# A recorded order of 2471 operations replaced by another: sliding-window attention and a token-mixing MLP on one core

## Chip, core and metric

The kernel runs on one NeuronCore of a Trainium2 chip. The metric is device time in microseconds (us), the median over several runs. The engines are named as the profile names them: PE (TensorE, matmuls; PEld its weight loads), DVE (VectorE), ACT (ScalarE), POOL (GpSimd) and SP (SyncE, whose queue issues every DMA here).

## What is computed

The input x is 2048 tokens of 512 features. The program runs two layers; each is an attention block and then a token-mixing MLP, both with a residual.

```python
def A(x):    # 32 heads of 16, window 256
    q, k, v = split(x @ wqkv)
    p = softmax(where(0 <= i - j < 256, q @ k.T / 4, -1e9))
    return (p @ v) @ wo
def B(x):    # mixes tokens: 2048 -> 1792 -> 2048, per feature
    u = gelu(einsum("sd,sf->df", layernorm(x), w1) + b1)
    return (einsum("df,fs->ds", u, w2) + b2).T
for _ in range(2):
    x = x + A(layernorm(x))
    x = x + B(layernorm(x))
```

## The kernel before

**Recording and replay.** The program isn't issued as it is written. Each call of `op(...)` puts an operation with its tiles, its engine and its possible other engines (`alts`) into a graph (L107 to L148). `replay` (L175) then goes through a list that `begin_order` decodes from the string `ORDER`: each entry names the operation that is next and which of its alternatives is used. The entries of one engine, in that sequence, are that engine's instruction stream; buffers of the pools (eight PSUM banks, seven `pt` tiles, and so on) are handed out in the same sequence. `emit` (L196) puts in the semaphore waits. So the string alone sets the order on every queue and the choice of engine.

**Work of a layer.** Tokens go in 16 tiles of 128. For each tile DVE takes statistics (`stat` L470, `agg` L472), POOL the power -0.5 (`rstd`, L483), and DVE normalises (`xh`, L490). The result is transposed into `xhT`: for the first four tiles on PE (`ftr`, L548) with a copy out of PSUM (`evt`, L555 on DVE or L557 on ACT), for the others by DMA (`tr`, L541). Projections are groups of matmuls on L512 (`fq`, `fk`, `fv`), evicted as `evq` (L571/L573), `evk` to a staging tile (L593/L595), `evka` straight into the block-diagonal keys `kbd` with two instructions (L582/L581), and `evv` (L630/L632). Staged keys are spread into `kbd` by `kz` on POOL or DVE (L608, two instructions) or by eight DMAs (L603). `kbd` has to be zero elsewhere: POOL fills two of its three slots at the start (`zero`, L460, 128x2048 each).

**Attention** goes over 152 groups of scores, 76 a layer. A group is `sc` on PE (L689, four row groups at once, two pairs of PSUM banks), two `exp` on ACT (L704, one for each pair of banks), up to a few `mask` operations on the edge blocks (L725: on POOL a product with `ldm`, on DVE an AND with `ldn`), and, once the groups of an output are there, `pv` (L746). The output is transposed by DVE (`od` L766), its reciprocal taken (`rec` L770), multiplied (`prod` L772, POOL or DVE), transposed back (`od2` L777), and goes through `fwo` (L512) and the residual `res` (L788).

**MLP.** `fu` (L512) and `ful` (L867) are the first product, part of it run during attention on the tokens that are ready; `evu` (L852/L854/L856) and `addu` (L878) gather it, `gelu` is on ACT (L882), `fy` (L512) is the second product and `resy` (L908, L894) its residual. Weights w1 and w2 stream in by DMAs of 128 KB (L802, L814).

**Start.** Before the first scores: POOL builds `ident`, `tri`, `mhalf`, sets the ones of `vst` (`one`, L457) and makes the two zero fills; PE runs 42 warm-up matmuls (L393); two tiles of x are normalised (`xh[48]` and `xh[44]`, the numbers being places in the recording), transposed (`ftr[51]`, `ftr[49]`), copied (`evt[52]` on ACT, `evt[50]` on DVE), and the first keys and queries are made from them (`fk[53]`, `fq[55]`), evicted, and used by `sc[113]`.

Of the kernel before, what the change touches and what calls it, by code (L numbers as in the profile page):

```python
# [14 lines left out]
ORDER = (
    'c-pO2F^KC{7QM2c=j(6YfM!uZS>AxMXh91KD2oCLD4;@F9MA^^T)0r-!i5VL+TcP9VsW7bFL*%#7cNvd;KGFiUhskg4!D?wSul$i9GJqz6cd=jg^MYsm|ga2'
    'Jmc}qpHF_Wku6K_>b<9X&b{|s3((~u28fD9C#cz^(P&uU6DaxBQmLft&MVz<4C52s)D1{l?kfP#BbAEk)EtMLm&@L%<IYdr`FswtJTWaWnS9KcJW&)X%U3)b'
    '@oN$VXI3W(lMXv3@d>4I%QDizq2cv9>WB4uy%I)YSkW{}gD9vq>L!28TupO`S}dvsCNn}ri4aOgJQ0AvsIVN~Twl`}&!;{9^74}Kq!YK3a=9Eg8-gHgmceFy'
    'IzQ!$hqIY|wmNgV7VtcOrO4Ci{CY93R1|+Un<+dGQaVk0-Sv8{5tW>uM^LW=gD@;NW{t+|L{*(?L05D#==IaVkT{g4N!s0bZQ>T<RvgO-fgk|UthU>2k>_hv'
    '4CixFCNo;ENu*Y<5yvSzm1<==^$2031}XbxJKjvzgTXZDo1Ry#_C9eeJ4#HyVtbzMnw5`Vxuw$l=5yEkcw?HbXCf-e)K$|mNyfw^XIaD1Xb6M%4bwE=6-7Y+'  # L20
    '_!A)@Nm8RB1|s8Yc+Yssxvn5O%h7Ua7=}<J7Z>odP|&otrnl#9nE}8N_=l9zUKB-e4M`G)n@vbzy^f;q&YEXu-=)!I=Q4rZ$;E25`p3yhr_(8~PCU;rPEJlw'
    '=imNrKCjme`+QoReLbDe|Fx0j>DfR$!&lbk^IF$5jHHt!ecy=VP8=Hsa`l%ujxDRzZbfmdP^yO!6;;<&#j0K1SY{b>k)HE>7@f(>KLnVLrCO~7P{z{%r#Nt3'
    '*XvT6fQ^Sl=@%dH(i{OxM3{^x;^+tvk|I*Z+O6YOb_hZn_$H=1GUn6*{IyIlN+rjkwHl>J1g~p~Q*?`(q`-!;%L~(zR%-ykWI$)b8G#Al-tS_D%ZhxMBnc!2'
    'XXw!&62kQ5;b8$-Gm=9lm(WdICkSS-$T?EIQYC(=EQ*SPg@Q49?>+R6ke9#+yY@F5K<b4fSfTYu)8?7)yeJ;RXhg?o8VrOq6$Pn7kJ`{$E-sMe>;*6x00*Nq'
    'P5W2<6hPB-LflfdR0)E*2QuaZRKfRjQ7eI7)K#E7D4>d00$4IwV#QyY5+HWw01WM++aD81hgLdBv1lw$FSgxw9P5#8=tiwrtGfnoFEvXyHQl3f*-&)e_g5o+'
    '2<^T^#Y!aF7&$2nf;0_+K&mTojG;0RO_2@(e4lBW<}##E#WQA2N|JCeX!qM~gwfW<@wf?ptA<KX5HPC~{1uCmbmUvU5Joy<S-kC9pjVH8RBP2MzQanq@ba_I'
    'sPHKpIQ?~>je#tPX%WN1go}m5Fn(M7upYMR1efCJ6<qUur)YSdXFI0tSg0@}pyp^AC-BI<KnZ>CrXf<QYU%|XsjJlj@6M6&nW|0H$%Ov~j&V&^Z?QNW27*fI'
    'g<4iCP3=FMjnjd{?|D9oczo{rd>Nn=ND^F0P`SDyqCgm<LV;f{m;8m5Z8BLdmes|g*PG24Ti7<UrWoDv`0L43f?o=r09=~(`n^t?{;Hkef_}e`jzS+ruzPiN'
    'NgyKa^YbwLGnN!PJ!uHdFpxqi(?hW;3as1x-1q$!iy`pC(02prGo@0gmMs8_d_+Xz*ovZXAIa})SOo}F(*f}@e91xua(ar<5Cu9KjbON5Gr5zrTkX-Zuvjeq'
    '-9izTW2p%sigPdd0;G43L?M|ZtUVmcxJkoxU)A79Qhly)wm_G(6Yck!uviR-!^N_U^pJ1ymC<-KvVT1uL%)xD?eU!sm-bTBEdyM)*Xy-q`Kz|n9pVO^WYF*5'  # L30
    '+~~cYjM}YrP_kRCd5GbjhH(?@z_wAAA*=B!k+EyJD4dS%6X#;NbR3y7Lz+lgHZVt$W!b>O(J<9eFBletgQ6fvD2|MQC<zh@3_qR1f2W41>q9aa47--z{{S?A'
    'gwHBnYO@xI%>Wnh6`@!J-nA)~yP}8%;o`D?-tVto9+JbCol{il)_6L@#>;&b^?QgArd<jskV!BKf@UG=_njW<TG6jyEg^c#0NwWy4R%DgNHwjiqSZ81Lq*Q3'
    'Olq(?T;sl_Tiq#sf4RQAz%}|tpD*-(o}+4?pO#@Z|7J45Ed0AT9*;#$6Gy80Wil%JX;)0KmnDhv<zF$W|A?LlLIAZ|Eeu1;bY1L<m27LbWV?2W5P?ufvOh)5'
    '&_4u1jy3f+1D-D&3&N2g5YjAgz4L}5qc$~8qF@qanTibxFzr3d!DTDa!iFrK0?5<eB)wihD3M!5i^AK_WCTg4EcSw4(g>3v3F2~qVeeIYmeA>T{G?O$TT65#'
    'TjdmCP_%8wE|qC{<JG*HYc`7IYR#;am}Qub;y4%y-A2}Q^hFd!))`Yl6$IJtg2Ed-Ntq;<WUuDjR3v|MO*hsRZ#bSLuASM<+4Sa;v1^Gj;pY0n5n`jWT3wKH'
    '8p^V^-gs-*9Z;UkVbN?h75?Uikg>Ny&w6l*e=?>Rm$Bg)ktbA%R?`4mA8(q9!Rs=Rl7{NzWKwM-M@S396KO=wc=$;N$Ni`Y*&u6waPZ93gS|zs?MrUIcMtD&'
    '+D^=d`P&ix=JR*veE!7?ynFFt_vrp|dy-qj!R_>eH~O(19z3=lWZ&H=x4jg0)ARWp<Z=&Bb|i4mQd77?nj<-qLAk?~eRA9rF1QzO!}uE`u|LQkJh5i4<{n%<'
    'czEq|@5^Q1J%G7f2052|!pbg4<S8RRkS*L3=JHz$_tVioe-xgz=AX5q_grqz$J}jz9=Ws&Ajdt}x3-5M-i|ZAavb--`+Z*T;6K{-O~v-JvBAO5N-TZLS@ao}'
    'bK7*fKX#`5t#jL)yHCAbZok;zox&qvWE%j0ci!2L5#AAQA3i=HnaFeZQuB-ZX_+}wnL7o_uK9faK~M6qQ>Q(Z;W!>IkM$@2WY!kQ!=nczx&6v|HX9!ebGiN1'
    '2r~C5W1gv-+kS>_XNU<hL3Tp>-0{e~CEy-XeoICngH*`BRy~FMQ_G$qzr&x~2l5!@y(zb^HuuqoyM)<;`M8jND6_GQ?@Nz+b1mG>;db5UbxnVp3fgURmy)|p'  # L40
    '?p)yDuA^}e%Fpe~A@?Yx+v!^o;hqS{Pwo}@|EIxlZ}ne*dz&8hLut?b7{B(Y-v8t9aL?T_xn=)OB<^E@zqxy|cbdJO{#3f}^5XvTv#Rv{@jteS6(a'
)
# [945 lines left out]
```

## Time and profile before

| | us |
|---|---|
| median of 3 runs (439.57 to 442.05) | 440.72 |
| the profiled execution's own time | 439.72 |
| its span, first to last instruction | 438.0 |
| PE busy / DVE / ACT / POOL | 422.0 / 324.0 / 315.4 / 187.8 |
| first `exp` of layer 1 starts | 12.36 |
| last `exp` of layer 1 ends (its table load follows at once) | 156.3 |
| last `fy` matmuls | to 435.0 |

The span has five stretches. Up to 12.36 us the first tiles are made ready. To some 156 us is the attention of layer 1, with the early part of the MLP in between. To some 200 us is the rest of the MLP of layer 1. To 358 us is the attention of layer 2, mixed with the last `fy` of layer 1 and the early MLP of layer 2; the rest is the MLP of layer 2. PE's busy time counts a matmul from issue to its modelled end, so that neighbours overlap. An instruction on ACT that lasts 1.05 us lets the next start 0.90 us after it began; the difference is overlap too.

### The profile page before, as it was taken

Reading aid. Unit: us, or ns where it says so; the run is one execution under the profiler, and the core shown is the slowest. Engines: PE = TensorE matmul, PEld = TensorE weight load, DVE = VectorE, ACT = ScalarE, POOL = GpSimd, SP = SyncE. Lnnn points to the kernel's source line nnn. Section 1 sums busy time; section 2 is a strip of 40 time slices with the busy share of each in tenths; the row PEclk is TensorE's granted clock in tenths of the full one; section 3 lists DMA queues with packets and bytes.
Section 4 is the critical chain, followed back from the end, with each engine's and each line's share of the span. In section 5 each row is a group of like instructions: output and inputs, shape, how many; then the busy total and the mean of one; then the engine's idle time right before and its main releaser. Section 6 shows DMA issues by size and latency. Waiting matters only on the chain.

```text
span 438.0 us, 13924 instructions
## 1 busy us (share of the span) xinstructions
PE 422.0 (96%) x5976; PEld 187.2 (43%) x5976; DVE 324.0 (74%) x634; ACT 315.4 (72%) x360; POOL 187.8 (43%) x278
## 2 busy tenths in 40 slices
PE   6989988999989999999999999999999999999997
PEld 5543433333434444444344444444444444444443
DVE  6999888988988679565677999989888757520214
ACT  2999999999999932704989999999999980520000
POOL 6779976548582421010255554468556411000000
PEclk8999999999999999999999999999999999999999
DMA  8745552212252635643583152122324134668513
GB/s 235 151 88 76 136 100 65 67 22 55 46 131 54 165 84 169 180 123 85 143 127 86 36 131 69 22 62 41 73 50 121 53 100 131 192 187 244 159 36 120
DMA packets 106668, 46.13 MB, mean 105 GB/s; under 512 B 36848, under 2 KB 106608, under 8 KB 106608
## 3 DMA queue, kind: packets, MB, share of 16 engines
q1 hardware_dynamic: 106608, 45.26, 42.0%
q8 instruction: 47, 0.77, 0.8%
q14 instruction: 13, 0.11, 0.1%
HBM read 33.56 MB, written 2.10 MB: 81 GB/s over the span
## 4 chain that ended last, share of the span: by engine, by line
PE 81%; ACT 13%; DVE 4%; issue 1%; POOL 1%; DMA 0%
PE PS L512 56%; ACT pt L704 13%; PE PS L689 9%; PE PS L867 8%; PE PS L746 7%; DVE xh_sb L490 1%; DVE stats L470 1%; DVE x_sb L788 1%; DMA x_sb<-in_A_x_dram 0%; POOL pt L725 0%; DVE kbd L582 0%; DVE rl L766 0%; DVE agg L472 0%; DVE stg L593 0%; DVE qT L571 0%
## 5 line engine op out<-in xcount | busy, mean ns | idle before, releaser
L704 ACT ACTIVATE pt<-PS 128x1024 bf16<-128x1024 f32 (+1 forms) x304 | 280.6, 1039 | 9.8 <-PE PS L689 8.9
L725 POOL TENSOR_TENSOR pt<-pt,ldm 128x256 int32<-128x256 int32 (+2 forms) x195 | 130.5, 689 | 106.1 <-ACT pt L704 105.6
L512 PE MATMUL PS<-xhT,wqkv 128*128 128x512 bf16 (+1 forms) x288 | 68.2, 363 | 2.0 <-ACT pt L704 0.9
L512 PE MATMUL PS<-xh_sb,w1b 128*128 128x512 bf16 x280 | 69.6, 381 | 0.3 <-issue 0.2
L512 PE MATMUL PS<-uT,w2b 128*128 128x512 bf16 (+1 forms) x294 | 68.5, 370 | 0.0
L689 PE MATMUL PS<-qT,kbd 32*128 32x256 bf16 (+4 forms) x1488 | 60.4, 252 | 5.0 <-ACT pt L704 1.4
L908 DVE SCALAR_TENSOR_TENSOR x_sb<-PS,b2col,x_sb 128x512 bf16<-128x512 f32 x31 | 22.8, 745 | 43.7 <-PE PS L512 43.6
L483 POOL TENSOR_TENSOR rstd<-agg,mhalf 128x2 f32<-128x2 f32 (+1 forms) x33 | 22.9, 695 | 63.4 <-DVE agg L472 63.3
L689 PEld LDWEIGHTS PS<-qT,kbd 32*128 32x128 bf16 x1488 | 21.9, 93 | 63.4 <-ACT pt L704 44.6
L766 DVE STREAM_TRANSPOSE rl<-PS 128x1024 f32<-128x1024 f32 x32 | 39.8, 1243 | 10.5 <-PE PS L746 10.5
L882 ACT ACTIVATE uT<-rl,b1col 128x512 bf16<-128x512 f32 x28 | 18.2, 712 | 38.5 <-DVE rl L878 38.3
L746 PE MATMUL PS<-pt,vb 64*17 64x320 bf16 (+4 forms) x2976 | 43.3, 252 | 1.6 <-POOL pt L725 0.6
L470 DVE BATCH_NORM_STATS2 stats<-x_sb 128x6 f32<-128x512 bf16 x64 | 42.9, 682 | 1.4 <-DMA x_sb<-in_A_x_dram 0.6
L512 PEld LDWEIGHTS PS<-uT,w2b 128*128 128x128 bf16 x294 | 27.1, 98 | 31.6 <-issue 3.7
L512 PE MATMUL PS<-uT,pt 128*128 128x512 bf16 x168 | 40.4, 380 | 0.0
L725 DVE TENSOR_TENSOR pt<-pt,ldn 128x256 int32<-128x256 int32 (+1 forms) x75 | 28.7, 404 | 15.7 <-ACT pt L704 15.5
L746 PEld LDWEIGHTS PS<-pt,vb 64*17 64x17 bf16 x2976 | 30.8, 85 | 17.7 <-ACT pt L704 6.1
L867 PE MATMUL PS<-xh_sb,w1b 128*128 128x512 bf16 x168 | 37.7, 379 | 0.0
L512 PEld LDWEIGHTS PS<-xhT,wqkv 128*128 128x128 bf16 x288 | 24.6, 99 | 29.7 <-issue 5.6
L512 PEld LDWEIGHTS PS<-xh_sb,w1b 128*128 128x128 bf16 x280 | 23.4, 97 | 31.9 <-issue 7.2
L512 PE MATMUL PS<-wqkv,xhT 128*128 128x512 bf16 x128 | 34.1, 381 | 0.0
L512 PE MATMUL PS<-wo_sb,oT 128*128 128x512 bf16 x128 | 32.3, 380 | 0.7 <-ACT pt L704 0.5
(61 smaller groups left out, 338.1 us busy)
## 6 DMA issues: line engine op xcount, KB each, us to landing
w1b<-in_B_w_dram SPq DMA_DIRECT2D x112, 128.0 KB, 2.9
w2b<-in_B_w_dram SPq DMA_DIRECT2D x70, 128.0 KB, 2.9
pt<-in_B_w_dram SPq DMA_DIRECT2D x42, 128.0 KB, 2.8
vb<-vst SPq DMA_DIRECT2D x64, 68.0 KB, 2.1
out_dram<-x_sb SPq DMA_DIRECT2D x15, 128.0 KB, 1.8
x_sb<-in_A_x_dram SPq DMA_DIRECT2D x3, 512.0 KB, 7.5
kbd<-stg SPq DMA_DIRECT2D x88, 16.0 KB, 1.9
wqkv<-in_A_wqkv_dram SPq DMA_DIRECT2D x4, 256.0 KB, 4.2
```

The lines of the kernel that those rows point to most:

```text
L470: op("vector:stat", lambda e: e.bn_stats(st[:, 0:6], x_sb[:, t, :]), reads=[f"x{t}"], writes=[("st", i)], cost=dve_cost(512))
L483: op("gpsimd:rstd", lambda e: e.tensor_tensor(rstd[:, t0:t1, 0], agg[:, t0:t1, 1], mhalf[:, 0:1].to_broadcast([P, t1 - t0]), op=ALU.pow), ...
L490: op("vector:xh", lambda e: e.tensor_scalar(xh_sb[:, t, :], x_sb[:, t, :], agg[:, t, 0:1], rstd[:, t, :], op0=ALU.subtract, op1=ALU.mult), ...
L512: return e.matmul(o, lhsT=w, rhs=x, start=start, stop=stop, skip_group_check=True)
L689: last = e.matmul(bank(tt[r // 2], r % 2)[:, base + c0 * 64:base + (c0 + n) * 64], lhsT=kbd[32 * r:32 * r + 32, tk.slot, o, jj].rearrange( ...
L704: op("scalar:exp", lambda e, ts=ts, tp=tp, i=i, cols=cols: e.activation(probs(tp)[:, i, 0:cols, :], pair(ts)[:, :, 0:cols].rearrange("p r ...
L725: return e.tensor_tensor(v, v, m, op=by)
L746: last = e.matmul(bank(t, h)[32 * r:32 * r + 17, i + q0 * 64:i + (q0 + n) * 64], lhsT=vb[64 * h:64 * h + 64, tk.slot, jj, 4 * o + r, :], r ...
L766: op("vector:od", lambda e, t=tod, tr=tr: e.transpose(rl[:, tr.slot:tr.slot + 2].rearrange("p a b -> p (a b)"), pair(t)), reads=[(tod, i) ...
L867: last = e.matmul(bank(tu, tt), lhsT=v()[:, sc - b0, k0 + tt * P:k0 + (tt + 1) * P], rhs=xh_sb[:, sc, :], start=(sc == b0), stop=(sc == NT ...
L882: op("scalar:gelu", lambda e, ft=ft, tt=tt: e.activation(uT[:, ft, :], rl[:, tmps[tt].slot], ACTF.Gelu_apprx_tanh, bias=b1col[:, ft:ft + 1 ...
L908: op("vector:resy", lambda e: e.scalar_tensor_tensor(x_sb[:, t, :], bank(ft), b2col[:, t:t + 1], x_sb[:, t, :], op0=ALU.add, op1=ALU.add), ...
```

## The change

The string `ORDER` is replaced; nothing else in the file differs.

```diff
 ORDER = (
-    'c-pO2F^KC{7QM2c=j(6YfM!uZS>AxMXh91KD2oCLD4;@F9MA^^T)0r-!i5VL+TcP9VsW7bFL*%#7cNvd;KGFiUhskg4!D?wSul$i9GJqz6cd=jg^MYsm|ga2'
...
+    'c-p;JL5S<t6}_^b=Rdb^Km%_;1qJkr0t%=_0Tukg1%2?s1qbwt0}8m{g$fS1Ac|7F@WKHX6mUQb2efd(3oRV*!T~S5_zM?YaA7`p;l*D}VF)gG@fTjqVkood'
...
 )
```

Decoded, the two lists hold the same 2471 operations. The start of the two, engine by engine (`-` and a number in brackets are nameless set-up operations: 0 to 2 `ident`, 3 `mhalf`, 26 and 27 the memset and the select of `tri`, 28 to 33 the mask tables `ldm` and `ldn`, 22 to 25 `par` and `half`, 37 to 39 the constants of `stats`):

```
POOL before: -[0] -[3] -[1] -[2] zero[35] rstd[47] -[26] rstd[43] -[27] one[34] zero[36] kz[66] rstd[83] mask[121] kz[71] kz[76]
POOL after:  -[3] -[0] -[1] -[2] one[34] zero[35] rstd[47] rstd[43] -[26] -[27] zero[36] rstd[83] kz[66] mask[117] kz[71] kz[76]
DVE before:  ... xh[48] xh[44] -[28] -[29] evt[50] -[31] -[32] -[30] ldn[33] evq[56] stat[81] stat[79] evq[68] evk[75] agg[82] evk[70] agg[80] evq[78] xh[84] evq[73] xh[85] stat[160] stat[153] evv[62] evt[87] evt[89]
DVE after:   ... xh[48] -[39] xh[44] stat[79] evt[50] -[28] stat[81] -[29] agg[82] agg[80] -[31] -[30] xh[85] -[32] ldn[33] xh[84] evq[78] evt[89] evk[70] stat[153] stat[160] stat[162] evt[87] ... evv[59] -[20] evv[62]
ACT before:  evt[52] evka[54] evk[65] exp[114] exp[115] exp[120] exp[119] exp[124] exp[125] evv[59] 3 exp evq[93] 5 exp evv[96] exp[232]
ACT after:   evt[52] evka[54] evq[56] evk[65] evq[68] exp[114] exp[115] evk[75] evq[73] 10 exp evka[102] 2 exp evv[96] exp[231]
PE before:   warm ftr[51] ftr[49] fk[53] fq[55] fk[64] sc[113] fq[67] fk[74] fk[69] sc[118] fq[77] fq[72] sc[123] 4 fv sc[133] ftr[86] ftr[88] sc[138]
PE after:    warm ftr[51] ftr[49] fk[53] fk[64] fq[55] fq[67] sc[113] fq[77] ftr[88] fk[69] fk[74] fq[72] sc[118] sc[123] ftr[86] 2 fv sc[133] 2 fv sc[138]
SP before:   x tile 1, x tile 0, wq (first half), wk (first half), x tiles 2-3, wk (rest), wq (rest), wv, x tiles 4-7, ...
SP after:    x tile 1, x tile 0, x tiles 2-3, wk (first half), wq (first half), wq (rest), wk (rest), x tiles 4-7, wv, ...
```

Over the whole program these operations change engine:

| kind | from | to | how many |
|---|---|---|---|
| `mask` | POOL / DVE | DVE / POOL | 49 / 37 |
| `prod` | POOL / DVE | DVE / POOL | 7 / 6 |
| `kz` | DMA | POOL | 6 |
| `kz` | POOL | DVE / DMA | 2 / 1 |
| `kz` | DVE | DMA / POOL | 2 / 1 |
| `evq` | DVE / ACT | ACT / DVE | 6 / 2 |
| `evk`, `evka` | DVE / ACT | ACT / DVE | 4 / 2 |
| `evv` | DVE / ACT | ACT / DVE | 1 / 4 |

So DVE gets 12 masks more than before (87 in place of 75), POOL 12 fewer (183 in place of 195). On PE the 152 groups of scores stand in the same sequence in both lists. In layer 1, from the 5th group of scores to the 73rd, the same amount of other PE work stands ahead of each fourth group; in layer 2 it differs by up to three matmul pairs. After the last `pv` of each layer the `ful` and `fy` operations stand in another order. The DMAs of w1 and w2 are spread differently over the queue of SP.

More of the change, by code (lines that the diff above doesn't have):

```diff
@@ L15 @@
 ORDER = (
-    'c-pO2F^KC{7QM2c=j(6YfM!uZS>AxMXh91KD2oCLD4;@F9MA^^T)0r-!i5VL+TcP9VsW7bFL*%#7cNvd;KGFiUhskg4!D?wSul$i9GJqz6cd=jg^MYsm|ga2'
-    'Jmc}qpHF_Wku6K_>b<9X&b{|s3((~u28fD9C#cz^(P&uU6DaxBQmLft&MVz<4C52s)D1{l?kfP#BbAEk)EtMLm&@L%<IYdr`FswtJTWaWnS9KcJW&)X%U3)b'
-    '@oN$VXI3W(lMXv3@d>4I%QDizq2cv9>WB4uy%I)YSkW{}gD9vq>L!28TupO`S}dvsCNn}ri4aOgJQ0AvsIVN~Twl`}&!;{9^74}Kq!YK3a=9Eg8-gHgmceFy'
-    'IzQ!$hqIY|wmNgV7VtcOrO4Ci{CY93R1|+Un<+dGQaVk0-Sv8{5tW>uM^LW=gD@;NW{t+|L{*(?L05D#==IaVkT{g4N!s0bZQ>T<RvgO-fgk|UthU>2k>_hv'
@@ L20 @@
[L20 to L39, printed above, removed]
@@ L40 @@
-    '2r~C5W1gv-+kS>_XNU<hL3Tp>-0{e~CEy-XeoICngH*`BRy~FMQ_G$qzr&x~2l5!@y(zb^HuuqoyM)<;`M8jND6_GQ?@Nz+b1mG>;db5UbxnVp3fgURmy)|p'
-    '?p)yDuA^}e%Fpe~A@?Yx+v!^o;hqS{Pwo}@|EIxlZ}ne*dz&8hLut?b7{B(Y-v8t9aL?T_xn=)OB<^E@zqxy|cbdJO{#3f}^5XvTv#Rv{@jteS6(a'
+    'c-p;JL5S<t6}_^b=Rdb^Km%_;1qJkr0t%=_0Tukg1%2?s1qbwt0}8m{g$fS1Ac|7F@WKHX6mUQb2efd(3oRV*!T~S5_zM?YaA7`p;l*D}VF)gG@fTjqVkood'
+    'mB*g(Oy;LaoAe4<?>)Wubnm(Mp8MQqi~#^?)ct(k%7f#1UbR|vD;4+mbnZa8Y#1LHLt_w|My>+puYwo0-Fl&~RysX*ePY=!oN~pQSXSZrU@{mCVj>x4J}>rr'
@@ new lines @@
+    'KxA3Gro+)tW+Lb3{G4o}C_Y>G-7u5`J{^%cX|>!|(=d*i@qVk@FpLp(97k1)looZJXj;ZFj8ak6BuOQNb0TuQrt9hSf-;(&0;+#?eRXx!W$}h{p0pjOQK{7&'
+    '&QBRNU%w{H*DzU~7bcU*Y(67oem1XG&&dj|uN7xFh+%!biU$K3B#74QbrV!j0{_qMa;X5!8w;>%^}6}8K2nJiS1OUv?aFc#A!g)L()zUBZZ_MEMn>#*yPt@J'
+    'P_floEQm8_PFW(HRJKwmd|0VgCKE!*ZwBRZZa6GjlepM_ma15lD9T%wWr9;K+jh<@m5QZjCA(x7&4OuK1*;I{Sw8xjv0N@UmgV6EfUdKNHHJI|)VvS9W7h4c'
+    'nyw{U5s)MaQF2`u5E9O4v3Op@fu%6lv?*@5T7lZl>c-PWCev<n5Jg}>DS+?$oonGL@VtwQ)*J8qAI&B-UiBAeYY4;DYPMR>{x(Ai!}3|MER{;H7K^26E|!bB'
@@ new lines @@
+    'SzDcrEO)lJw$A>w36%INNgBodVH_jyrs<l)>af!>E2i1$gw0OavF#{|a*TPV*JwA4W~<3`-!FZv6{=dJ+2CATbH+XIqvf((cDGV41C*u!P7#KT#l>QYmHs&B'
+    '7E4923I?T2dir!O$&|mGygcO-!01r95-Z)1y(5b4pxtUgyN%B#5X*vky>3}~tHN{jT#ZwzGmVP4i7K1s5yl-sU_@1$zcxVuf_F9^#T$Jpt+QfJR^;%w(>V=0'
+    ';kbj!YTAkKdmVhXTv|=sa7s=xY;xh*w#}F+QC-(1g~vIP4JF93Y%(XVM<kn(E*$_aiWf;ZFLa$t8@`r!(i31fq;!bE9`$+@eMB*MgKTCppTC}?IWU_I0Q&t{'
+    '=tKYP93YnqI>Fg8h%pY@woaf97}182L=UJ2r?M*N2*|*FA6Q~np4W-$)-Y253YFOm3XTjmv4W0KFf1zwY_nuTl8vrbHl18KuW1FdW9qu8X~lv_F)?zOo2*)h'
@@ new lines @@
+    '8r@2WLDZHQt<@N<y49ds#kIQad3CX_>or$LE0jc3CJ*IANOw5&!>})@!*;s{uG?(-{=f^p5ZBTsM;I9WET3o0_gNOVuN#J$xSP@B3zD>9RaUGN%R`hC=eSUg'
+    'B<cC{d{4@kn@y+uYtLiMF55v69KTm~%6^risQ_iBYAOn2?<h<OWKHLqC_cq)k4;JR*k+??>otCAjguGe>W2PqW-=a2(r}0am}J3d)bv@$Fl!=aeq~^c;AgR!'
+    'GclJ?S~OcZY5mn<{6lgqeL!oH3nILELolkSkXbAi7ijz&vRI6l=gZ*&!T7uU&U89MM}aXO!7pL-<!A_`gn{xoL_Nd!BGg7|sE1*|<38d-`Z16z-fWUU2r;e~'
+    '3%}L!eMw^VvCn;vNkK3idR`pIt-zfJQOKD1JFi}CVn~+Vx>IsqyeM&QB^(v94#Nb)xEFJxY6w>VnrayDfyR*t=kpmtb$SdZgE-z8X0)c^Ke>o5iRtBKh>*OA'
@@ new lines @@
+    'RatJe<V8rxpQfBN5TRKVsbt(Dyd4t|>IHGdjx!&b%=qmLHJPZ(*Goa^_mwk}nazqtfUm6a&k<dU5lxFRJ|OJrfXw!}g#_D0IvZl@e?bQW5q+q~L2t8>8*m9s'
+    'Rdp{oZ!eafH%BOf7UV#P4MlgWWxRBBpRN}mA&bQKrahZUrt}NwYG2BrD3EWMem;lHiD?HIp%RxQphyF<LatHZic6e|S67#Ov-x^F9*el6*zad!O=r*vL);aC'
+    'LJj|b<)@}lMLw1o&nrqcCnheZU2?WKLnBUT2VjH(qePXzKrgC~>&S+q&ybQJ==A&jkFg>YYt@?5Xf#aI1jBS|06i=ShM_UH&@n?9BbUPo=C>#^hRP*`&qRi_'
+    'EJ<!lwl7wMmcU}KAoprDpH0uF(<xn?k;#;xYrY&$#-p)hNIF(+i29nw1FI6MpLT+zYWSa^l0m!najk}IY}zIiQMoecmi564cy57>s>|{-$X(=~J$wHbGsC<f'
@@ new lines @@
+    '1k>P5?hE|%ROocYV?0_&By-UrzL1~_B)LUA3?NWc%o&O@n<)ypsCaea%RV%xQPiXfD1h}KsJX3P8v*m14If;<LrD|yX=<*EwUu+HA9Jv6GS!f!3PCRK<*s@_'
+    '^Y|5$VFt+!BcCr~d3DU9t*SO!t%Zh!X|8B8WkX~%1BsPM3()9%GnedhQJjhtQ*=fy>hQ8o^q1g{#-mHvY{<*#`g$E*4x{Tnxl)}T9#n|aA;>E8S-u?F%}KE+'
+    '+p63Gg%`v^qan$%U-!Iz6U%l^#sfy7VBtZgR>MHghgMz&8Otj$TPzXA9GX{EliYAe;!~{3Kw-;NKZXc`fIqOkg>B<j$b$~O*H3zxo8<)d3%6Ym2od&O9C!lo'
+    'BpFZN?w-c$R?<(>yWW%i-Xwib$0ImOr&2fVR62EZ_-6P1cH^Vl(Z>b%Nj*dW?%RDZzJo^C-g}$2R;KPo9;_A!kSF^l5roHK|32=y(`M@<VgK{EfjcV?O-^i1'
@@ L42 @@
+    'Wm4Z%0Cg4cPCZ!hHZUG4ev6#&HW1-~Bh&CB%K_d=@TC%*Qo=28!U3Sd&bN0fQoHxUZ6qHg$K6`t(eFLxX+aQv5TihV|F@(ckF0GtC9)5!o6deLb(dy`@t1le'
+    '^zXy@(>>gK9Fu=AH_uxF5_WiE(EemgJNS;=&=lD!yd{$Co$~1i2Bp*4<Tv^9_IWU2-%8)(rc~-6hjtKblj-g0a)`io>dn{=u|r25hU$JKu@)^C$kEZx@cpdB'
+    'TH%hA$%B$`-_-PhVd<UiH=RsoH@2IRNpE@l@x)9WHd5d8?4x$?_+}5<wv*l?CM1{(JAM})aIf&~c`e)$jqrF%2>*M!9nkIJZriqSr!(C3g}vf}aF1OMIp*NH'
+    'H}B?=2J%({`8G*?9|HMqMMwD0dI<j=8Gkno50O47F%RnOV_FLLRTIAT8#_XWTbKT@)cJ2+HxhX'
 )
```

## Prediction

> **What bounds the kernel.** I read the page first, then the stretches, then the waits, then the first 26 us as a timeline.
>
> ```profile
> span 438.0 us, 13924 instructions
> PE 422.0 (96%) x5976; PEld 187.2 (43%) x5976; DVE 324.0 (74%) x634; ACT 315.4 (72%) x360; POOL 187.8 (43%) x278
> PE 81%; ACT 13%; DVE 4%; issue 1%; POOL 1%; DMA 0%
> ```
>
> PE is the bound, and ACT carries 13% of the chain that ended last. The stretches (columns: PE, PEld, DVE, ACT and POOL busy, granted clock, DMA share, GB/s) say where:
>
> ```profile
> 5.31:8.72 3.41, 0.92 (x13) 0.57 (x10) 3.24 (x4) 0.58 (x1) 2.62 (x4) 1.00 0.95 275
> 8.72:12.13 3.41, 3.08 (x24) 1.94 (x24) 2.02 (x8) 1.13 (x3) 0.00 (x0) 0.50 0.93 230
> 20.00:40.00 20.00, 17.22 (x447) 9.15 (x450) 19.44 (x48) 19.14 (x24) 16.80 (x25) 1.00 0.39 74
> 40.00:156.00 116.00, 110.82 (x2076) 44.86 (x2069) 98.87 (x187) 113.61 (x123) 72.99 (x105) 1.00 0.38 84
> 200.00:358.00 158.00, 157.64 (x2644) 66.29 (x2643) 128.92 (x251) 149.48 (x168) 79.92 (x116) 1.00 0.35 79
> 358.00:435.00 77.00, 76.96 (x370) 35.91 (x370) 30.39 (x51) 10.59 (x17) 1.38 (x2) 1.00 0.52 150
> ```
>
> From 40 to 156 us ACT is busy 98% and PE 96%: the exponentials set the pace, one each 0.90 us from start to start, and PE waits for banks. From 200 us PE has no gap worth the name. So time can be won in three places: before the first exponential, in what interrupts ACT in layer 1, and hardly after 200 us.
>
> ```profile
> ACT pt L704 <- PE PS L689: 8.9, 25, 0.8
> POOL pt L725 <- ACT pt L704: 105.6, 68, 7.7
> ```
>
> ACT's interruptions in its main work are 8.9 us in all over both layers (first line: total, times, longest). POOL waits 105.6 us for exponentials (second line): moving masks off POOL relieves an engine that idles for most of the run.
>
> The start, POOL and then DVE (start, duration, ...):
>
> ```profile
> 4.76 0.63 POOL L483 TENSOR_TENSOR rstd<-agg,mhalf 128x1 f32<-128x1 f32 x1
> 5.36 0.29 POOL L442 TENSOR_SCALAR_AFFINE_SELECT tri<-tri 128x128 bf16<-128x128 bf16 x1
> 5.59 0.64 POOL L457 MEMSET vst<- 128x128 bf16 x1
> 5.83 2.10 POOL L460 MEMSET kbd<- 128x2048 f32 x1
> ```
>
> ```profile
> 4.59 0.38 DVE L490 TENSOR_SCALAR xh_sb<-x_sb,agg,rstd 128x512 bf16<-128x512 bf16 x1
> 5.43 2.65 DVE L490 TENSOR_SCALAR xh_sb<-x_sb,agg,rstd 128x512 bf16<-128x512 bf16 x1 [0.46 <-POOL rstd L483]
> ```
>
> The same instruction takes 0.38 us and then 2.65 us. The second ran beside a select, a memset and the second zero fill on POOL, and ended at 8.08, just after the fill (7.93). Work on POOL held it back some 2.25 us, and the chain of waits goes through it: `ftr[49]` starts at 8.14.
>
> **The start in the new order.** POOL now does `one[34]` (0.64) before the first fill: 1.66 + 0.64 + 1.80 = 4.1, then `rstd[47]`, 0.14 later than before; `rstd[43]` waits for `agg[42]` (4.68) and stays at 4.76 to 5.39. So `xh[44]` asks at 5.43 as before. What runs on POOL then is the memset of `tri` (0.20, 5.36 to 5.56); its select waits for it, and between two such dependent instructions POOL left 0.07 us (1.35 to 1.42 for the selects of `ident`). Behind the select comes the 2.1 us fill. If DVE gets in at 5.56, `xh[44]` ends at 5.9, 2.15 us earlier; if not, at about 8.0, as before. I take the first: elsewhere in the trace normalisations and masks on DVE that met a POOL mask (0.7 us) were held by that one alone (0.80 to 0.86 in place of 0.41), even with the next mask right behind. [...]
>
> Then: `ftr[49]` at 5.97 (2.17 us earlier), `evt[50]` behind one `stat` (0.68) at 6.45 to 6.87, `fk[53]` at 6.95 in place of 9.05. Its weights are now the fourth DMA; the fourth landed at 5.57, the fifth and sixth at 7.6 and 8.3, in time for `fq[55]`, now third. Four groups in place of three stand ahead of `sc[113]`: at the cold rate of the 8.72 stretch (12 matmuls 2.6 us, 0.85 a group) it starts at 10.4, at the warm rate (0.44 a group), with `evka[54]` (0.84) and `evq[56]` (0.43) in turn on ACT, at 9.0; before, 11.73. The cold stretch follows one in which PE was busy 0.92 of 3.41 us; now that would be some 2.2. [...] It decides little: `evk[75]` waits anyway for `fk[74]`, which stands behind `ftr[88]`, `xh[85]`, `rstd[83]` and so the fill's end (8.0 + 1.2 us of statistics + 0.7 + 0.4, up to 0.4 more beside `kz[66]`): about 12.2. So `exp[119]` comes at 13.0 in place of 14.7 (its pair began at 14.19): **1.2 us won**.
>
> ACT from there to its 15th exponential:
>
> ```profile
> 12.36 4.89 ACT L704 ACTIVATE pt<-PS 128x1024 bf16<-128x1024 f32 x6 [0.16 <-PE PS L689]
> 17.14 0.60 ACT L632 CAST vst<-PS 128x512 bf16<-128x512 f32 x1
> 25.65 1.02 ACT L704 ACTIVATE pt<-PS 128x1024 bf16<-128x1024 f32 x1 [0.67 <-PE PS L689]
> ```
>
> Before, 14 exponentials, two `evv` and one `evq` took 13.3 us with a hole of 0.9 ahead of 25.65 that ends when DVE delivers `evq[108]` (25.14). After, from `exp[119]`: 8 x 0.90 + 4 x 0.48 + `evka[102]` 0.85 + `evv[96]` 0.47 = 10.4, so 23.4. DVE has to follow: from 20 to 40 us it is busy 19.44. Counted by the list up to the 17th group of scores it has 40.7 us of work before and 40.8 after, but now it loses no 2.25 us to the fill; adding its rows up from 8.0 us (with 0.09 overlap each) gives `evq[104]`, which the 15th exponential now needs, at 23.0, so 23.6. **2.0 us won at that point**, and DVE some 3 us ahead of where it was.
>
> **The rest of layer 1.** ACT's pace is the same and the order of the groups too, so the 2.0 us pass through to the end at 156 us, unless holes open or close. From 27 to 57 us POOL had, by the list and the rows (0.727 and 0.455 a mask of 256 and 128 columns, 1.06 a `prod`, 1.38 a `kz`), 27.5 us of work in 30; now 23.7, DVE 31.2 for 33.2. The holes there sum to 1.4 us, those to 156 us to 3.3. I count 0.5 of these 4.7 as closed (bounds: 2.0 closed, or 1.0 more). The 49 masks that go to DVE cost 0.42 or 0.28 each there, the 37 others and the evictions pay back, and DVE gains 3.5 us over the whole span: hidden under ACT and PE (DVE has 17 of 116 us free from 40 to 156). Without that cover it would be at most those 3.5.
>
> **After 156 us.** PE runs without gaps and its work is the same. Two covers could fail. The `ful`/`fy` order changed: the shortest way from a `ful` to the `fy` that needs its gelu was 2.0 us, now, counted in matmul pairs of 0.43, 3.6: no stall. Weights: three w2 tiles near 390 us wait for later `addu` and by the median 2.9 us to land arrive some 0.7 us before need (closest before: 0.8). Without that margin, under 1 us each. Both taken as 0 (bounds -0.5 to +1.5), as are the pair moves in layer 2, where ACT's holes are as large as before.
>
> **Sum.** Against the profiled execution, 439.72: -2.0 - 0.5 = 437.2. That execution was 1.0 under the median of 440.72, so **438.2 us**.
>
> **Rivals.**
> - *POOL isn't free at 5.56* (the change does not do what its words say). `xh[44]` ends at 8.0 again. Then the fourth group ahead of `sc[113]` costs 0.8 and ACT's extra evictions before the 15th exponential (13.0 us of work for 12.15) 0.85, with nothing to pay them: +1.65, **442.4**, slower. It decides as soon as memset, select and fill hold DVE as one run, which is what the old row shows for select, memset and fill. Against it: only the dependent pair has a gap.
> - *The start is won and eaten in layer 1*: masks on DVE meet POOL's and `od` is late by one mask (0.42) here and there; each hole of 0.3 to 0.4 that opens ahead of a `pv` takes from ACT. Five of them: +1.75, so **440.0**. For it: DVE's 19.44 of 20. Against it: POOL is less loaded.
> - *Holes close too*: DVE's 3 us lead takes away 2 us of the holes and the warm start holds: **436.0**. For it: several of the waits from 22 to 57 us end on DVE's evictions and `od`.
>
> **Chances.** Forecast 0.58, first rival 0.17, second 0.15, third 0.10. The third and the lower bounds set the low end, 435.6; the upper end, 441.7, takes in the second and half of the first. A measurement here can tell about 0.5% (2.2 us) from no change; the forecast lies 2.5 us under, so about two thirds of it counts as faster: faster 0.38 + 0.10 = 0.48; same 0.20 + 0.13 + 0.09 (first and second rival) = 0.42; slower 0.04 + 0.06 = 0.10, where these two come together or the second is twice its size.
>
> **What will show it.** Right: in the new timeline the second `xh` is under 0.7 us, `ftr[49]` starts near 6.0, the 15th exponential near 23.6, and the last exponential of layer 1 ends near 153.8. Wrong: an `xh` of 2 us or more at 5.4; or a 15th exponential at 23.6 with the end of layer 1 unmoved; or gaps of PE after 200 us, above all at 376 to 400 us with a DMA as releaser.

## The result

| | median, us | lowest to highest | ratio to before, 95% interval |
|---|---|---|---|
| before, 18 runs | 440.4 | 438.53 to 442.78 | |
| after, 18 runs | 437.8 | 436.83 to 440.21 | 0.9946 [0.9932, 0.9960] |

The new order is 0.5% faster; 438.2 had been forecast. The page of after (span, busy time, chain by engine):

```profile
span 438.5 us, 13838 instructions
PE 412.4 (94%) x5909; PEld 186.3 (42%) x5976; DVE 324.1 (74%) x641; ACT 316.7 (72%) x364; POOL 182.6 (42%) x273
PE 68%; ACT 22%; DVE 3%; DMA 2%; issue 2%; SPq 1%; POOL 0%
```

Two things about this page. The profiled execution took 440.21, the highest of the 18, so its span says little of the gain. And 67 of 5976 matmuls have no record, so its PE is too low. The same list was therefore profiled once more (`new_again`, 438.46 us):

```profile
span 436.7 us, 13905 instructions
PE 421.1 (96%) x5976; PEld 186.7 (43%) x5976; DVE 322.7 (74%) x641; ACT 316.4 (72%) x364; POOL 182.5 (42%) x273
PE 77%; ACT 14%; DMA 3%; DVE 2%; SPq 2%; issue 1%
```

Busy times are those of before but for POOL (187.8 then): the work is the same, so the time came from waits. The start in after, POOL and then DVE:

```profile
4.00 1.25 POOL L483 TENSOR_TENSOR rstd<-agg,mhalf 128x1 f32<-128x1 f32 x2
5.20 0.20 POOL L441 MEMSET tri<- 128x128 bf16 x1
5.48 0.37 POOL L442 TENSOR_SCALAR_AFFINE_SELECT tri<-tri 128x128 bf16<-128x128 bf16 x1
5.79 1.80 POOL L460 MEMSET kbd<- 128x2048 f32 x1
```

```profile
5.28 0.41 DVE L490 TENSOR_SCALAR xh_sb<-x_sb,agg,rstd 128x512 bf16<-128x512 bf16 x1 [0.25 <-POOL rstd L483]
5.61 0.69 DVE L470 BATCH_NORM_STATS2 stats<-x_sb 128x6 f32<-128x512 bf16 x1
6.22 0.41 DVE L555 COPY xhT<-PS 128x512 bf16<-128x512 bf16 x1
6.54 1.10 DVE L444 TENSOR_SCALAR ldm<-tri,half 128x64 int32<-128x64 bf16 x1
```

The second `xh` is through in 0.41 us where it took 2.65. POOL leaves 0.08 us free between the memset of `tri` and its select, and `xh`, which began beside that memset, isn't held. The fill now holds another instruction, a builder of `ldm` (1.10 us; 0.23 before), but that one stands behind the copy (L555) on which PE waits. PE then makes the first keys and scores early:

```profile
5.76 0.40 PE L548 MATMUL PS<-ident,xh_sb 128*128 128x128 bf16 x4 [0.28 <-DVE xh_sb L490]
6.68 1.92 PE L512 MATMUL PS<-xhT,wqkv 128*128 128x256 bf16 x16 [0.53 <-DVE xhT L555]
8.63 0.40 PE L689 MATMUL PS<-qT,kbd 32*128 32x256 bf16 x12
```

The stretches of after at the start (columns as before: length, five engines, clock, DMA share, GB/s):

```profile
5.31:8.72 3.41, 2.57 (x27) 1.81 (x28) 2.96 (x10) 1.94 (x5) 2.71 (x4) 1.00 0.97 284
8.72:12.13 3.41, 3.02 (x52) 2.11 (x50) 3.14 (x9) 3.35 (x7) 2.21 (x6) 1.00 1.00 232
```

PE is busy 2.57 us of the first (0.92 before), and the second runs at the full clock (0.50 before). The trace of after holds no record of the clock, and a row without one shows 1.00; that the clock was full is read from the matmuls: 16 of the same shape take 1.92 us here, and 12 took 2.74 before. ACT in `new_again`, up to where the start's gain stands:

```profile
9.43 1.94 ACT L704 ACTIVATE pt<-PS 128x1024 bf16<-128x1024 f32 x2
...
21.70 1.94 ACT L704 ACTIVATE pt<-PS 128x1024 bf16<-128x1024 f32 x2 [1.36 <-PE PS L689]
23.52 0.60 ACT L632 CAST vst<-PS 128x512 bf16<-128x512 f32 x1
24.23 11.27 ACT L704 ACTIVATE pt<-PS 128x1024 bf16<-128x1024 f32 x12
```

The first exponential starts 2.9 us earlier than before, the 15th (24.23) only 1.4 earlier: a hole of 1.36 us has opened between them. The rest, in `new_again`, first the stretches and then the waits:

```profile
40.00:156.00 116.00, 111.70 (x2159) 45.83 (x2158) 97.51 (x185) 113.79 (x123) 70.87 (x104) 1.00 0.33 77
200.00:358.00 158.00, 157.15 (x2639) 65.73 (x2637) 129.84 (x259) 149.71 (x169) 76.51 (x111) 1.00 0.33 79
```

```profile
POOL pt L725 <- ACT pt L704: 86.1, 60, 5.3
ACT pt L704 <- PE PS L689: 9.9, 26, 1.4
```

ACT and PE are as full as before. POOL waits 19.5 us less for exponentials, since it has fewer masks, but ACT's interruptions have not become fewer (9.9 us; 8.9 before). The starts of a few exponentials in every profile, each from its own trace, show where each kernel gained or lost:

| kernel | 1st | 15th | 37th | last of layer 1 | span |
|---|---|---|---|---|---|
| before | 12.4 | 25.6 | 46.4 | 155.2 | 438.0 |
| after | 9.1 | 24.1 | 46.1 | 155.0 | 438.5 |
| new_again | 9.4 | 24.2 | 45.1 | 153.2 | 436.7 |
| start_new_rest_old | 9.3 | 22.7 | 43.8 | 153.4 | 435.8 |
| start_old_rest_new | 12.4 | 25.8 | 50.1 | 158.4 | 441.8 |
| start_old_again | 11.3 | 26.1 | 49.4 | 158.5 | 442.0 |
| setup_only_new | 9.7 | 23.0 | 46.3 | 155.1 | 437.9 |
| setup_rest_new | 9.7 | 23.0 | 47.2 | 156.0 | 439.4 |
| pool_moves_only | 11.8 | 25.1 | 45.9 | 156.3 | 439.2 |
| fills_behind | 13.2 | 27.4 | 48.3 | 156.4 | 439.9 |
| fills_chained | 9.7 | 23.9 | 44.8 | 152.9 | 436.5 |
| fills_on_act_old | 9.5 | 22.7 | 43.5 | 152.3 | 435.0 |
| fills_on_act_new | 9.5 | 22.7 | 43.8 | 153.2 | 435.7 |
| w1_later | 9.1 | 23.9 | 44.7 | 152.8 | 436.3 |

A single span is one execution; the verdicts below go by the ratios.

### The profile page after: what moved, and what is told of

Read it like the earlier page. It is cut to its first block, busy times and chain, and to the rows that moved or that the text cites. A ratio compares the mean times of both kernels' runs of the same rounds, so it can differ in the third digit from the quotient of the medians.

```text
span 438.5 us, 13838 instructions
## 1 busy us (share of the span) xinstructions
PE 412.4 (94%) x5909; PEld 186.3 (42%) x5976; DVE 324.1 (74%) x641; ACT 316.7 (72%) x364; POOL 182.6 (42%) x273
## 4 chain that ended last, share of the span: by engine, by line
PE 68%; ACT 22%; DVE 3%; DMA 2%; issue 2%; SPq 1%; POOL 0%
PE PS L512 46%; ACT pt L704 22%; PE PS L867 8%; PE PS L689 7%; PE PS L746 6%; DMA x_sb<-in_A_x_dram 2%; SPq L410 1%; DVE xh_sb L490 1%; DVE stats L470 1%; SPq L406 0%; DVE pt L725 0%; DVE vst L630 0%; DVE rl L766 0%; DVE x_sb L788 0%; POOL pt L725 0%
## 5 line engine op out<-in xcount | busy, mean ns | idle before, releaser
L704 ACT ACTIVATE pt<-PS 128x1024 bf16<-128x1024 f32 (+1 forms) x304 | 281.2, 1041 | 12.6 <-PE PS L689 11.9
L725 POOL TENSOR_TENSOR pt<-pt,ldm 128x256 int32<-128x256 int32 (+2 forms) x183 | 119.9, 676 | 87.9 <-ACT pt L704 86.3
L512 PE MATMUL PS<-xh_sb,w1b 128*128 128x512 bf16 x265 | 66.6, 380 | 2.6 <-issue 1.6
L512 PE MATMUL PS<-xhT,wqkv 128*128 128x512 bf16 (+1 forms) x273 | 64.2, 355 | 4.2 <-ACT pt L704 1.5
L725 DVE TENSOR_TENSOR pt<-pt,ldn 128x256 int32<-128x256 int32 (+1 forms) x87 | 33.2, 401 | 8.3 <-ACT pt L704 8.0
L867 PE MATMUL PS<-xh_sb,w1b 128*128 128x512 bf16 x164 | 37.4, 379 | 0.2
L512 PE MATMUL PS<-wqkv,xhT 128*128 128x512 bf16 x117 | 31.8, 380 | 1.6 <-issue 1.1
L512 PE MATMUL PS<-wo_sb,oT 128*128 128x512 bf16 x120 | 31.2, 380 | 1.6 <-ACT pt L704 1.1
```

The source lines that it names most:

```text
L512: return e.matmul(o, lhsT=w, rhs=x, start=start, stop=stop, skip_group_check=True)
L704: op("scalar:exp", lambda e, ts=ts, tp=tp, i=i, cols=cols: e.activation(probs(tp)[:, i, 0:cols, :], pair(ts)[:, :, 0:cols].rearrange("p r ...
L725: return e.tensor_tensor(v, v, m, op=by)
L867: last = e.matmul(bank(tu, tt), lhsT=v()[:, sc - b0, k0 + tt * P:k0 + (tt + 1) * P], rhs=xh_sb[:, sc, :], start=(sc == b0), stop=(sc == NT ...
```

## The experiments

The theory: the whole gain is the hold of the second zero fill on `xh[44]`, taken away by where POOL's set-up stands. Its rivals: the rest of the new list (mask moves, evictions, order after layer 1) earns its share; or the start is won and eaten.

**The new list once more, and the two lists crossed.** `start_new_rest_old` takes the new list up to the 14th group of scores (some 36 us) and the old one behind it; `start_old_rest_new` is the reverse. Loads of w1 that only one of the two halves had ahead of the seam stand at the seam or behind it.

```diff
 order = new list
+        up to sc[264], then every operation not yet done, as the old list has them
```

> The new order once more, for a second profile: the first profile of it was its slowest execution of 18 (440.21 against a median of 437.8). Expected: 0.9946 of before, so 438.0 where before has 440.4. If the start is what pays, this profile has the first exponential near 9.1 us as in the first, and the three holes on ACT between 38 and 48 us (0.86, 0.83 and 0.68 us in the first profile) are smaller, so that the last exponential of layer 1 ends near 153.8 and not at 156.0. If they are as large, the 2.4 us come from somewhere behind 156 us.

Measured: 438.51 us, ratio 0.9959 [0.9943, 0.9974].

> The new order up to the 14th group of scores (some 36 us), the old one from there. Start theory: all of the gain, -2.0 to -2.5 us. Rest theory (the moved masks and evictions pay): within 0.7 us of before.

Measured: 437.62 us, ratio 0.9946 [0.9928, 0.9964]. The new start alone gives all of it; with the new rest behind it the time is 0.2 to 0.9 us longer (437.8 and 438.51), which the intervals do not separate from nothing. The traces do ("Behind layer 1", below).

> The reverse: the old order up to the 14th group of scores, the new one from there. Start theory: within 0.7 us of before. Rest theory: -1.7 to -2.4 us.

Measured: 443.96 us, ratio 1.0091 [1.0070, 1.0112]: 4.0 us slower than before, which no theory had expected. Its waits have a line that before does not have:

```profile
PE PS L512 <- DVE qT L571: 2.3, 1, 2.3
```

PE waits once, at 41.8 us, 2.3 us for one `evq`, and the 37th exponential is 3.7 us late; to the end nothing more is lost. Two explanations were open: the new list's order on DVE relies on the 3 us that DVE is ahead after the new start, or the two halves do not fit at the seam.

**Only seven set-up operations.** The old list, with nothing moved but these:

```diff
 POOL
-zero[35] rstd[47] -[26] rstd[43] -[27] one[34] zero[36]
+one[34] zero[35] rstd[47] rstd[43] -[26] -[27] zero[36]
 DVE
-xh[48] xh[44] -[28] -[29] evt[50]
+xh[48] xh[44] evt[50] -[28] -[29]
```

Seven entries stand elsewhere in the list; queue by queue only four operations change places: `one[34]` and `-[26]` on POOL, `-[28]` and `-[29]` on DVE.

> The old order with only its set-up moved: on POOL the ones of vst ahead of the first zero fill and the memset and select of tri behind the second rstd, and on DVE the two mask-table operations behind the copy evt[50]. If the normalisation held back by POOL is what cost the start: it lasts under 0.7 us in place of 2.65, the third PE transpose group of four starts near 6 us, the first scores near 9.6, and the whole gains 1.0 to 2.0 us, less than the full new start because DVE and ACT share the evictions as before. [...] If the other moves of the new start carry it, it gains under 0.5 us though the normalisation is short.

Measured: 437.71 us, ratio 0.9940 [0.9919, 0.9961]. This is the whole gain (2.6 us of 440) from seven moves; the other operations that the change moves add nothing that these times can show.

**The POOL half of it.** DVE keeps its old order.

```diff
 POOL
-zero[35] rstd[47] -[26] rstd[43] -[27] one[34] zero[36]
+one[34] zero[35] rstd[47] rstd[43] -[26] -[27] zero[36]
```

> The old list with the five moves on POOL alone (one[34] ahead of zero[35]; the memset and select of tri right behind rstd[43]; then zero[36]); DVE keeps the old order, so that the two builders of ldm, -[28] and -[29], stand ahead of evt[50] and -[28] waits for the select of tri. xh[44] should take about 0.4 us either way. If the fill's hold on xh is all that was lost, the DVE moves add nothing: ratio 0.994, as setup_only_new. If -[28] is then held by the second fill itself (it took 1.10 us in place of 0.23 there), evt[50] comes 0.7 to 1.5 us later than in setup_only_new and the ratio is 0.995 to 0.998.

Measured: 439.36 us, ratio 0.9974 [0.9953, 0.9995]. DVE's timeline in it:

```profile
5.43 0.41 DVE L490 TENSOR_SCALAR xh_sb<-x_sb,agg,rstd 128x512 bf16<-128x512 bf16 x1 [0.46 <-POOL rstd L483]
6.03 1.76 DVE L444 TENSOR_SCALAR ldm<-tri,half 128x64 int32<-128x64 bf16 x1 [0.18 <-POOL tri L442]
7.83 0.28 DVE L446 SCALAR_TENSOR_TENSOR ldm<-tri,half,ldm 128x64 int32<-128x64 bf16 x1
8.03 0.42 DVE L555 COPY xhT<-PS 128x512 bf16<-128x512 bf16 x1
```

`xh` is free, but the fill (5.94 to 7.74) now holds the builder of `ldm` for 1.76 us, and the copy that PE waits for stands behind it on DVE's queue: 8.03 in place of 6.52 in `setup_only_new`. So the hold has to go to an instruction behind which nothing urgent stands.

What the late copy costs goes with PE's clock in these runs. Each run lists the mean granted clock of its span, and the twelve runs of this kernel fall into two groups by it: five show 1.000 and took 437.8 to 438.5 us, seven show 0.992 to 0.996 and took 439.2 to 440.9. A stretch of 3.41 us at half clock in a span of 438 us makes 0.996. The profile is one of the seven and has that stretch:

```profile
4.72:8.13 3.41, 1.23 (x18) 0.88 (x16) 2.74 (x5) 0.58 (x1) 2.92 (x4) 1.00 1.00 283
8.13:11.54 3.41, 3.04 (x24) 1.94 (x24) 2.03 (x8) 1.10 (x3) 0.00 (x0) 0.50 1.05 271
```

At the full clock the kernel is near `setup_only_new`, whose five runs at 1.000 took 436.4 to 437.8 us. So most of what the POOL half alone loses, some 2.4 us between the two groups, comes with the halved stretch behind PE's wait; that the half clock is all of it isn't shown. The moves on DVE are needed so that PE doesn't stand idle so long (2.20 us ahead of the first keys in `pool_moves_only`, 0.52 in `setup_only_new`).

**What holds DVE.** Two kernels on the new list put the second fill elsewhere. In `fills_behind` POOL issues `one[34]` and the fill right behind `rstd[43]`, with no dependence between them; `fills_chained` makes the same fill wait for `one[34]`:

```diff
 POOL
-one[34] zero[35] rstd[47] rstd[43] -[26] -[27] zero[36]
+zero[35] rstd[47] rstd[43] one[34] zero[36] -[26] -[27]
 # fills_chained alone:
-               writes=["kz0"], cost=1900)
+               reads=["one"] if k == 2 else [], writes=["kz0"], cost=1900)
```

> The new order with one change on POOL: behind the second rstd come the ones of vst (0.65 us) and the second zero fill (1.8 to 2.1 us), which don't wait for each other, and the memset and select of tri go behind the fill. Run theory (a chain of independent fills holds DVE to its end): xh[44] asks near 5.3 us and ends with the fill, lasting 2.0 to 2.4 us, and the kernel loses most of its gain, 439.5 to 441. [...]

> The same, but the second fill waits for the ones (a semaphore between the two). Run theory: the gap lets DVE in, xh[44] lasts 0.7 to 1.1 us, and the time is again near 438. If xh[44] lasts over 2 us here as well, a gap of some 0.07 us isn't what frees it.

Measured: 441.04 us, ratio 1.0014 [0.9997, 1.0031], and 438.26 us, ratio 0.9954 [0.9936, 0.9971]. POOL and then DVE in `fills_behind`:

```profile
5.30 0.64 POOL L457 MEMSET vst<- 128x128 bf16 x1
5.54 2.10 POOL L460 MEMSET kbd<- 128x2048 f32 x1
```

```profile
5.39 2.41 DVE L490 TENSOR_SCALAR xh_sb<-x_sb,agg,rstd 128x512 bf16<-128x512 bf16 x1 [0.44 <-POOL rstd L483]
```

And in `fills_chained`:

```profile
5.35 0.64 POOL L457 MEMSET vst<- 128x128 bf16 x1
6.04 1.84 POOL L460 MEMSET kbd<- 128x2048 f32 x1
```

```profile
5.43 0.71 DVE L490 TENSOR_SCALAR xh_sb<-x_sb,agg,rstd 128x512 bf16<-128x512 bf16 x1 [0.44 <-POOL rstd L483]
```

The same two POOL instructions with one more wait between them: the fill begins before the memset is over (5.54 against 5.94) in the first and behind it (6.04 against 5.99) in the second; `xh` takes 2.41 or 0.71 us, and 2.8 us of the whole time hang on it (with the clock, which is halved for two stretches in the first profile and full in the second). So here two independent POOL instructions issued back to back held `xh` to the end of the last (the fill ends at 7.64, `xh` at 7.80), and a dependence between them let it in. As with the masks that the prediction cites, one POOL instruction alone held it in `fills_chained` (0.71: the rest of one memset); in `fills_behind` and before it was the next instruction too (2.41 and 2.65).

**The fills on ACT.** The two fills become activations with scale 0.0 on ACT (which in `pool_moves_only` idles 3.5 us ahead of its first copy, at 5.6 us), on the old list and on the new start with the old rest.

```diff
-            op("gpsimd:zero", lambda e, k=k: e.memset(kbd[:, k].rearrange("p a b c d -> p (a b c d)").bitcast(dt.float32), 0.0),
+            op("scalar:zero", lambda e, k=k: e.activation(
...
+                uT[:, 0, 0:P].unsqueeze(1).to_broadcast([P, 16, P]), ACTF.Copy, scale=0.0),
```

> The old order, with both zero fills done by ACT (a copy of ones with scale 0, some 1.8 us each, between its table load and its first copy, where it idles from 2.1 to 5.9 us). Nothing that takes over 0.7 us is left on POOL ahead of the scores. If the hold by the fill is the cause: xh[44] lasts 0.4 to 1.2 us and the old order gains what the new one did, 2.0 to 2.8 us (437.4 to 438.2). If the start's gain came from the other moves: under 0.7 us.

> The new start (to the 14th group of scores) with the old rest, and both fills on ACT. Start theory: the mask-table operation that POOL's fill still held for 1.10 us in the new order and the third rstd come earlier, so another 0.3 to 1.0 us: 436.6 to 437.4. If ACT is what bounds by then (its fills end at 5.7 and the first copy at 5.5 moves by 0.2), nothing more is won: 437.6 within 0.5.

Measured: 437.69 us, ratio 0.9929 [0.9908, 0.9949], and 437.76 us, ratio 0.9942 [0.9922, 0.9961]. The old list without any fill on POOL gains as much as the new one, and the new start gains no more from it. (The old list's `xh` still takes 0.95 us there, from 5.45 to 6.40, beside the select and `one`, which do not wait for each other; `one` ends at 6.26. That fits the same hold, by a shorter run.) The interval of the 0.9929 overlaps that of after's 0.9946: no kernel of this study is shown to beat after.

**Was it the lead or the seam?** `setup_rest_new` is `start_old_rest_new` with the seven set-up moves and nothing else; `start_old_again` repeats `start_old_rest_new` beside it.

> This is start_old_rest_new (old list up to the 14th score group, new list behind it; 444.0 us, ratio 1.0091, PE waiting 2.3 us for a qT at 41.8 us) with seven set-up operations put otherwise: on POOL one[34] ahead of zero[35], the memset and select of tri right behind rstd[43], then zero[36]; on DVE -[28] and -[29] behind evt[50]. Every other operation stands as there, the seam too. Lead theory (the new list's DVE order behind 36 us needs the 3 us by which DVE is ahead when the fill does not hold it): the qT wait goes, the 37th exponential starts at 45 to 47 us in place of 50.1, and the ratio is 0.993 to 0.998 (437.3 to 439.5 us). Seam theory (two halves of different lists do not fit together, whatever the lead): only the 2.6 us of the start come off, the wait at 41.8 us stays in some form, the ratio is 1.002 to 1.005.

> start_old_rest_new once more, on the chip of the two kernels above: old list up to the 14th score group, new list behind it. If its loss was of the kernel: ratio 1.007 to 1.011 and a wait of PE for qT of about 2 us near 41.8 us. If it was of that chip or of those executions: ratio near 1.000, no such wait.

Measured: 441.07 us, ratio 1.0019 [1.0003, 1.0035], and 444.55 us, ratio 1.0100 [1.0072, 1.0128]. The wait in `setup_rest_new`:

```profile
PE PS L512 <- DVE qT L571: 2.2, 1, 2.2
```

The loss repeats, and the wait stays when everything comes 2.8 us earlier (39.0 in place of 41.8 us). My theory of the lead falls: it is the seam. In the chain of `setup_rest_new` DVE works without a break from 33.98 to 38.96, and the late `evq` (38.39) is the last of it:

```profile
33.98 1.25 DVE rl L766
35.23 1.07 DVE xh_sb L490 x2
36.30 0.60 DVE stats L470
36.90 0.61 DVE oT L777
37.51 0.58 DVE stats L470
...
38.39 0.57 DVE qT L571
```

A hybrid of two orders can lose 4 us that neither list has; so `start_old_rest_new` says nothing of the new rest, for or against. `start_new_rest_old` has a seam too, and may hide a gain or a loss of the same kind, though the same line of its waits is 0.2 us; what carries the verdict on the rest is that `setup_only_new`, which has no seam, gets the whole gain.

**Behind layer 1.** From the end of layer 1's last exponential to the end of the span it is 281.3 to 281.8 us in the six profiles that have the old list there, and 282.4 to 282.7 us in the eight that have the new one. The ranges don't meet: the new rest costs some 0.9 us (the difference of the means) behind layer 1, too little for the times of the runs to show. Of this, 0.6 us is one wait of PE, which ends at 318.0 us in `new_again`, ahead of a `pv` whose exponential comes late. In the stretch from 200 to 358 us all eight have this line of waits, and none of the six:

```profile
PE PS L746 <- ACT pt L704: 0.6, 1, 0.6
```

**The hole ahead of the 15th exponential.** In `new_again` it begins with DVE, which waits for the last tiles of x:

```profile
17.51 0.69 DVE L470 BATCH_NORM_STATS2 stats<-x_sb 128x6 f32<-128x512 bf16 x1 [0.97 <-DMA x_sb<-in_A_x_dram]
```

`start_new_rest_old` has the same instruction at 16.31 without a wait, and its seam had moved three loads of w1 to a later place. So in `w1_later` only these three moved, on SP:

```diff
 SP (new list)
-... bst w1[506] vz[63] 4 tr vz[100] wo w1[538] w1[536] tr ...
+... bst vz[63] 4 tr vz[100] wo ... (behind sc[264]) w1[506] w1[538] w1[536] ...
```

> The new list with three loads of w1 moved on the queue of SP alone, from ahead of the 14th score group to right behind it, so that no w1 transfer stands among the last tiles of x, the first vst copies (vz) and the first transposes; every other queue is the new list's. In the new order DVE waits 0.97 and 1.19 us near 17.5 us for the last x tiles, and the 15th exponential starts at 24.1 to 24.2 us behind a hole of 1.35 us; in start_new_rest_old, where those loads stand later, it starts at 22.7 without that hole. If the early w1 load is what delays x: no such DVE wait, the 15th exponential at 22.5 to 23.0 us. If the 1.4 us then last to the end: ratio 0.991 to 0.993 (436.3 to 437.2 us). If they are taken back before 156 us by ACT's later holes, as it seems from the two kernels whose layer 1 ends at the same 154.4: ratio 0.994 to 0.996. If the load is not the cause: 15th exponential at 24.1 and ratio 0.9946 to 0.996.

Measured: 438.12 us, ratio 0.9945 [0.9923, 0.9967].

```profile
17.38 0.69 DVE L470 BATCH_NORM_STATS2 stats<-x_sb 128x6 f32<-128x512 bf16 x1 [1.20 <-DMA x_sb<-in_A_x_dram]
```

The wait is still there, and the 15th exponential at 23.9: the w1 load isn't its cause. What makes the last transfer of x land a microsecond earlier in some profiles stays open. It cost nothing that lasts: the last exponential of layer 1 starts at 152.8, in `start_new_rest_old`, without the hole, at 153.4.

## Why the prediction was right

**The start.** The path was the one foretold. `xh[44]` was to be done at 5.9 and was at 5.69; `ftr[49]` 5.97, came at 5.76; `fk[53]` 6.95, came at 6.68; `xh[44]` asked 0.15 us earlier than reckoned (5.28). Of the two starts of `sc[113]` (9.0 at the warm rate, 10.4 at the cold) the warm one came: 8.63, with 16 matmuls in 1.92 us. `evk[75]` was put at 12.2 and came at 11.0 in after, because the third `rstd` was at 8.22: `exp[119]` started at 11.7, not 13.0, so 2.5 us were won there where I had 1.2. Of the clock I had said that it decides little. The runs of `pool_moves_only` say more: 2.4 us lie between those at full clock and those with a halved stretch.

**The 15th exponential.** I had 23.6 with 2.0 won. In after and `new_again` it starts at 24.1 and 24.2 (1.4 to 1.5 won), in `start_new_rest_old` and `fills_on_act_new`, which have the new start and no wait for x, at 22.7 (2.9 won). The term left out was the arrival of the last tiles of x: I followed DVE by its rows alone, and DVE waited 0.97 to 1.2 us for a DMA. The two errors, ahead of it and here, nearly cancel, which is luck.

**The rest of layer 1.** "The 2.0 us pass through": yes. The end of layer 1 was put at 153.8 and came at 154.3 in `new_again` and 156.0 in after. "0.5 of the holes close": not shown; ACT's interruptions are 9.9 and 11.9 us in the two profiles, against 8.9, and the 1.36 us of the new hole is in them. After's profile has three holes of 0.7 to 0.9 us between 38 and 48 us which `new_again`, the same list, has not, and its layer 1 ends 1.7 us later; what made them in that execution stays open.

**After 156 us.** Put at 0, between -0.5 and +1.5. From the end of layer 1 to the end of the span it is 281.7 us before and 282.5 in `new_again`: +0.8, within the bounds, but no accident, since all eight profiles with the new rest show it. The order of the groups of scores hadn't changed, but the exponential ahead of one `pv` comes 0.6 us too late; gaps of PE after 200 us stood among the signs of being wrong, and there is one.

**The rivals.** The first (POOL not free at 5.56) is the one that the experiments made real. What it supposes happens in `fills_behind` (`xh` 2.41 us), and all of the gain is gone (441.04, ratio 1.0014); the loss of 1.65 us on top that I had put to it (442.4) is at the most 1.4 by its interval. It decided where the POOL instructions were independent (2.41 us there, 2.65 in before); in the new list the select needs the memset, and a gap of 0.08 us (0.05 in `fills_chained`) was enough. The second (start won, eaten in layer 1) isn't seen: the kernels with the new start and `xh` freed stay at 0.994 to 0.996. The third (holes close too) isn't seen. By the runs the sum is -2.6 for the set-up and about 0 for the rest, where I wrote -2.0 and -0.5. So the mechanism was right and its size too small; that the total came within 0.4 us of the forecast is in part luck.

## What to carry to other kernels

Where an instruction on DVE takes several times its usual length, look at what POOL runs beside it, and then at whether POOL's next instruction depends on the one before: here a dependence (`xh` 0.71 us in place of 2.41), or the fills moved to an engine that idled (0.95 in place of 2.65), freed DVE. Freeing it paid in full only where the next instruction to be held had nothing urgent queued behind it (ratio 0.9940 in `setup_only_new`, 0.9974 in `pool_moves_only`), so move both. Where PE has stood idle, look at its clock in the next microseconds too (0.50 in before, behind a stretch with 0.92 of 3.41 us busy). And of a reordering of thousands of operations a handful may carry the whole gain: take these alone onto the old list, and prefer that to crossing two lists, since a seam can cost more than either list (`start_old_rest_new` took 443.96 us, before and the new list beside it 440.08 and 438.51).
